# Row scalings moved to GpSimd, one weight load on ScalarE's queue, wider units for two features, and a new order

## The chip, the core and the metric

The kernel runs on one core of a Trainium2 chip. A core has five engines that work side by side and wait for each other through semaphores: TensorE (PE in the profile, with its weight loads as PEld), VectorE (DVE), ScalarE (ACT), GpSimd (POOL) and SyncE (SP), which issues most of the DMAs. The metric is the time of one execution on the device in microseconds (us). The kernel before takes 196.92 us, the median of three runs from 196.87 to 197.14.

## What is computed

The reference normalizes the rows of x (2048 x 640, bf16) and adds two branches to x: a spectral filter (a two-dimensional real FFT, a product with a complex weight, the inverse FFT) and a gated linear unit with 1536 features.

```python
xn = _layernorm(x, axis=-1)
# branch A, on xn
X = rfft2(xn)                    # 2048 x 321, complex
y = irfft2(X * (w_r + 1j * w_i))
# branch B, on xn
g = einsum("bsd,df->bsf", xn, w_gate)
u = einsum("bsd,df->bsf", xn, w_up)
z = einsum("bsf,fd->bsd", g * u, w_down)
out = x + y + z
```

## The kernel before

The 2048 rows are 16 row tiles of 128. Everything is cut into 959 small tasks. Each task has a name, an engine, and a function that emits its instructions; a table `_PLAN` (line 405) lists the tasks as triples of task number, engine (0 PE, 1 ACT, 2 DVE, 3 POOL, 4 SP) and PSUM bank. `replay` takes the table as it stands: each engine runs its tasks strictly in the listed order. `compute_waits` then adds the semaphore waits that the data, the buffers and the banks require. The durations written beside the tasks are estimates that `replay` adds up for a report and for ordering the waits; they are no instructions. So the order of each engine, and the engine of each task, are fixed by the table.

The stages, with the task names used below:

- **Normalization** (lines 731 to 798). A row tile b is loaded (`ld_x`), its mean and variance come from DVE (`bn`, `ag`, L754 and L761) or from two passes on ACT (`sm`, `sq`, L736 and L745). `sd` (ACT, L770 or L771) takes the square root, `rs` (DVE, L778) the reciprocal, for one row tile in groups 0 to 3 and for two in later ones, and `mul` (L795) writes (x - mean) * rs over the row tile in place: one instruction on 128 x 640 bf16 values.
- **Transposes**. Row tiles 0 to 3 are transposed on PE (`T0`, L814) and copied out of PSUM (`eT0`). Row tiles 4 to 15 are transposed by DMA from SP's queue (`xt`, L802), each behind its `mul`.
- **Gated unit, first half** (lines 926 to 996). A table `chunks` says which row tiles are multiplied with which features: an entry (b0, nb, f0, f1) covers nb row tiles from b0 and features f0 to f1 - 1, where one feature is a block of 128. With nb = 4 a unit is one feature with 512 columns, 5 matmuls for each of gate and up (`GU`, L951); with nb of 1 or 2 it is two features side by side, 10 matmuls of 128 or 256 columns (`GU`, L973). Two copies `eG` (ACT L681 or DVE L682) bring gate and up out of PSUM into one of three buffers, and `H` (DVE, L991 or L993) multiplies them. The weights arrive in pairs `ld_gw0_0` (gate) and `ld_gw0_1` (up), `ld_gw2_0`, and so on.
- **Forward spectral part**. On groups of 2, 2, 4, 4 and 4 row tiles DVE runs five steps `S1` to `S5` (L857 to L892), 12 instructions that combine columns of the normalized rows with two inputs from SBUF each; `S1` waits for the `mul` of all row tiles in its group and for that of the row tile behind it (row tile 3 for the first group). `R` (PE, L905) multiplies the result of a row tile, and `eR` copies it out. Then come `D` (L1034), `C` (L1053), the product with the complex weight `WM` and `SM` on DVE (L1070 to L1087), four copies with a sign `JA` to `JD` (L1100), of which `JC` and `JD` run on POOL, and `IA` (L1116).
- **Inverse part and output**. `I` (L1144), five DVE steps `V1` to `V5`, the second half of the gated unit `ACC` (L1221), which accumulates with `IV` (L1233) in one bank, and the final copies, additions and stores.

At the start PE runs 45 matmuls on constants (`warm`, L714), then `T0_0`, five more on constants (`fill0`, L704), and the first `GU`. On SP the first loads stand in this order: the first half of row tile 0 (the second half is on ACT's queue), row tile 2, row tile 1, `ld_gw0_1`, row tile 3, `ld_gw0_0`, `ld_gw2_1`, `ld_gw2_0`. On DVE the first tasks are `bn0`, `bn0`, `ag0`, `rs_0`, `mul0`, `bn1`, `bn1`, `ag1`, the two copies of `T0_0`, `rs_1`, `rs_2`, `mul1`, `mul2`. On ACT they are `sd_0`, `sm2`, `sq2`, `sd_2`, `sd_1`, `sm3`, `sq3`, `sd_3`. All sixteen `mul` run on DVE.

Of the kernel before, what the change touches and what calls it, by code (L numbers as in the profile page):

```python
# [376 lines left out]
def _d_mm(n):  # L377
    return max(n, 64) / 2.4 + 2.5
# [6 lines left out]
def _d_dve_psum(n):  # L385
    return n * 1.04 + 70.0
# [6 lines left out]
def _d_dve_tt16(n):  # L393
    return n * 0.52 + 68.0
# [6 lines left out]
def _d_act(n):  # L401
    return n * 0.833 + 62.0
# [3 lines left out]
    (11, 4, -1), (18, 2, -1), (10, 0, 2), (12, 1, -1), (0, 3, -1), (8, 3, -1), (19, 2, -1), (20, 2, -1), (21, 1, -1),  # L406
    (22, 2, -1), (23, 2, -1), (14, 4, -1), (36, 1, -1), (37, 1, -1), (38, 1, -1), (13, 4, -1), (28, 2, -1), (27, 2, -1),
    (29, 2, -1), (30, 1, -1), (24, 0, 6), (26, 2, -1), (25, 2, -1), (9, 0, 2), (31, 2, -1), (39, 2, -1), (32, 2, -1),
    (40, 2, -1), (170, 4, -1), (181, 0, 7), (15, 4, -1), (43, 1, -1), (44, 1, -1), (45, 1, -1), (33, 0, 5), (35, 2, -1),
    (34, 2, -1), (169, 4, -1), (172, 4, -1), (171, 4, -1), (16, 4, -1), (182, 1, -1), (46, 2, -1), (47, 2, -1), (41, 0, 3),  # L410
    (179, 0, 2), (180, 1, -1), (183, 2, -1), (112, 2, -1), (173, 4, -1), (174, 4, -1), (191, 0, 4), (192, 1, -1), (42, 1, -1),
    (189, 0, 1), (190, 1, -1), (48, 0, 2), (49, 1, -1), (186, 0, 5), (187, 1, -1), (196, 0, 4), (197, 1, -1), (193, 2, -1),
    (113, 2, -1), (194, 0, 7), (195, 1, -1), (62, 1, -1), (184, 0, 2), (185, 1, -1), (54, 2, -1), (53, 2, -1), (188, 2, -1),
    (17, 4, -1), (51, 2, -1), (55, 2, -1), (50, 2, -1), (52, 2, -1), (63, 1, -1), (64, 1, -1), (56, 1, -1), (114, 2, -1),
    (57, 2, -1), (198, 2, -1), (115, 2, -1), (204, 0, 3), (206, 0, 6), (65, 1, -1), (199, 0, 4), (205, 1, -1), (66, 1, -1),
    (207, 1, -1), (60, 2, -1), (116, 2, -1), (200, 1, -1), (201, 0, 7), (202, 1, -1), (203, 2, -1), (58, 2, -1), (209, 0, 0),
    (210, 1, -1), (72, 1, -1), (1, 4, -1), (211, 0, 6), (212, 1, -1), (121, 2, -1), (208, 2, -1), (67, 2, -1), (213, 2, -1),
    (119, 0, 2), (122, 2, -1), (70, 2, -1), (176, 4, -1), (175, 4, -1), (73, 1, -1), (7, 4, -1), (120, 1, -1), (117, 0, 4),
    (123, 2, -1), (216, 0, 1), (214, 0, 7), (118, 1, -1), (74, 1, -1), (217, 1, -1), (215, 1, -1), (75, 1, -1), (76, 1, -1),
    (218, 2, -1), (124, 2, -1), (68, 2, -1), (77, 2, -1), (78, 2, -1), (177, 4, -1), (221, 0, 2), (219, 0, 3), (125, 2, -1),  # L420
    (82, 1, -1), (224, 0, 0), (178, 4, -1), (220, 1, -1), (222, 1, -1), (225, 1, -1), (226, 0, 4), (227, 1, -1), (223, 2, -1),
    (83, 1, -1), (229, 0, 6), (230, 1, -1), (228, 2, -1), (130, 2, -1), (69, 4, -1), (61, 4, -1), (128, 0, 1), (129, 1, -1),
    (84, 1, -1), (231, 0, 5), (232, 1, -1), (233, 2, -1), (131, 2, -1), (85, 1, -1), (86, 1, -1), (234, 0, 4), (235, 1, -1),
    (236, 0, 2), (241, 0, 7), (242, 1, -1), (237, 1, -1), (92, 1, -1), (126, 0, 5), (239, 0, 3), (240, 1, -1), (87, 2, -1),
    (238, 2, -1), (132, 2, -1), (243, 2, -1), (133, 2, -1), (90, 2, -1), (134, 2, -1), (93, 1, -1), (94, 1, -1), (244, 0, 4),
    (59, 4, -1), (71, 4, -1), (251, 0, 1), (245, 1, -1), (95, 1, -1), (127, 1, -1), (249, 0, 0), (250, 1, -1), (96, 1, -1),
    (246, 0, 3), (247, 1, -1), (248, 2, -1), (97, 2, -1), (80, 2, -1), (254, 0, 7), (255, 1, -1), (252, 1, -1), (253, 2, -1),
    (98, 2, -1), (100, 2, -1), (88, 2, -1), (256, 0, 6), (257, 1, -1), (139, 0, 4), (141, 0, 2), (142, 1, -1), (259, 0, 0),
    (140, 1, -1), (137, 0, 1), (138, 1, -1), (3, 4, -1), (258, 2, -1), (432, 4, -1), (468, 4, -1), (431, 4, -1), (260, 1, -1),
    (143, 2, -1), (261, 0, 6), (262, 1, -1), (102, 1, -1), (263, 2, -1), (144, 2, -1), (135, 0, 3), (266, 0, 5), (267, 1, -1),  # L430
    (269, 0, 7), (264, 0, 1), (103, 1, -1), (271, 0, 2), (276, 0, 0), (104, 1, -1), (265, 1, -1), (268, 2, -1), (145, 2, -1),
    (136, 1, -1), (105, 1, -1), (270, 1, -1), (277, 1, -1), (272, 1, -1), (440, 4, -1), (274, 0, 3), (281, 0, 4), (279, 0, 1),
    (79, 4, -1), (473, 4, -1), (106, 1, -1), (273, 2, -1), (433, 4, -1), (89, 4, -1), (5, 4, -1), (434, 4, -1), (91, 4, -1),
    (2, 4, -1), (467, 4, -1), (4, 4, -1), (282, 1, -1), (107, 2, -1), (146, 2, -1), (110, 2, -1), (441, 4, -1), (101, 4, -1),
    (439, 4, -1), (435, 4, -1), (438, 4, -1), (472, 4, -1), (442, 4, -1), (286, 0, 4), (81, 4, -1), (147, 2, -1), (280, 1, -1),
    (275, 1, -1), (278, 2, -1), (108, 2, -1), (283, 2, -1), (156, 2, -1), (287, 1, -1), (284, 0, 5), (285, 1, -1), (148, 0, 2),
    (154, 0, 6), (150, 0, 0), (151, 1, -1), (149, 1, -1), (289, 0, 4), (290, 1, -1), (294, 0, 1), (295, 1, -1), (152, 0, 2),
    (291, 0, 0), (292, 1, -1), (153, 1, -1), (288, 2, -1), (296, 0, 1), (297, 1, -1), (301, 0, 4), (302, 1, -1), (157, 2, -1),
    (293, 2, -1), (158, 2, -1), (298, 2, -1), (159, 2, -1), (160, 2, -1), (299, 0, 1), (300, 1, -1), (155, 1, -1), (306, 0, 5),
    (304, 0, 0), (307, 1, -1), (305, 1, -1), (303, 2, -1), (311, 0, 1), (312, 1, -1), (309, 0, 5), (310, 1, -1), (161, 0, 3),  # L440
    (163, 0, 1), (164, 1, -1), (308, 2, -1), (162, 2, -1), (314, 0, 7), (165, 0, 4), (166, 2, -1), (315, 2, -1), (167, 0, 2),
    (316, 0, 0), (317, 2, -1), (168, 1, -1), (443, 0, 1), (446, 0, 3), (445, 1, -1), (444, 2, -1), (477, 0, 5), (447, 1, -1),
    (479, 1, -1), (321, 0, 7), (322, 1, -1), (478, 1, -1), (448, 2, -1), (313, 2, -1), (318, 2, -1), (324, 0, 1), (325, 1, -1),
    (99, 4, -1), (466, 4, -1), (109, 4, -1), (436, 4, -1), (470, 4, -1), (497, 4, -1), (437, 4, -1), (451, 0, 3), (452, 2, -1),
    (319, 0, 0), (320, 1, -1), (449, 0, 5), (450, 2, -1), (323, 2, -1), (453, 2, -1), (457, 3, -1), (455, 2, -1), (498, 4, -1),
    (469, 4, -1), (111, 4, -1), (471, 4, -1), (503, 4, -1), (474, 0, 1), (476, 1, -1), (456, 3, -1), (475, 1, -1), (502, 4, -1),
    (454, 2, -1), (326, 0, 7), (327, 1, -1), (329, 0, 0), (330, 1, -1), (505, 0, 1), (507, 1, -1), (506, 1, -1), (334, 0, 3),
    (508, 0, 6), (331, 0, 4), (510, 1, -1), (509, 1, -1), (482, 0, 1), (483, 2, -1), (336, 0, 0), (480, 0, 5), (481, 2, -1),
    (328, 2, -1), (484, 2, -1), (332, 1, -1), (335, 1, -1), (337, 1, -1), (344, 0, 7), (345, 1, -1), (536, 0, 2), (538, 1, -1),
    (537, 1, -1), (429, 4, -1), (460, 0, 1), (458, 0, 4), (341, 0, 0), (342, 1, -1), (459, 1, -1), (504, 4, -1), (333, 2, -1),  # L450
    (485, 2, -1), (486, 2, -1), (461, 1, -1), (464, 0, 7), (465, 1, -1), (462, 0, 5), (339, 0, 6), (340, 1, -1), (463, 1, -1),
    (349, 0, 0), (350, 1, -1), (501, 4, -1), (530, 4, -1), (499, 4, -1), (500, 4, -1), (511, 0, 1), (513, 0, 3), (567, 0, 6),
    (568, 1, -1), (569, 1, -1), (514, 2, -1), (512, 2, -1), (351, 0, 5), (352, 1, -1), (515, 2, -1), (516, 2, -1), (346, 0, 0),
    (347, 1, -1), (528, 4, -1), (564, 4, -1), (532, 4, -1), (430, 4, -1), (562, 4, -1), (535, 4, -1), (531, 4, -1), (559, 4, -1),
    (529, 4, -1), (561, 4, -1), (533, 4, -1), (534, 4, -1), (487, 3, -1), (488, 3, -1), (489, 0, 7), (495, 0, 6), (338, 2, -1),
    (490, 1, -1), (517, 2, -1), (594, 4, -1), (591, 4, -1), (6, 4, -1), (596, 4, -1), (539, 0, 4), (343, 2, -1), (565, 4, -1),
    (541, 1, -1), (496, 1, -1), (359, 0, 3), (491, 0, 2), (492, 1, -1), (540, 1, -1), (360, 1, -1), (493, 0, 7), (356, 0, 0),
    (357, 1, -1), (494, 1, -1), (354, 0, 2), (355, 1, -1), (544, 0, 3), (542, 0, 0), (601, 0, 5), (602, 1, -1), (603, 1, -1),
    (543, 2, -1), (366, 0, 7), (367, 1, -1), (545, 2, -1), (348, 2, -1), (546, 2, -1), (548, 2, -1), (547, 2, -1), (381, 0, 2),
# [62 lines left out]
def _build(nc, A_x, A_w_r, A_w_i, B_w_gate, B_w_up, B_w_down, out, opts=None):  # L522
    opts = opts or {}
# [821 lines left out]
```

## Time and profile before

| what | value |
|---|---|
| median of three runs | 196.92 us |
| the profiled execution | 196.79 us |
| span of its trace | 195.1 us |
| granted TensorE clock | 1.0 |
| matmuls of 128x512 in L951 | 420, mean 379 ns |
| matmuls of 128x256 and 128x128 in L973 | 160, mean 246 ns |
| `mul` (L795) on DVE | 16, mean 437 ns |
| H (L991) on DVE | 42, mean 427 ns |
| L1100 on POOL, 64x252 bf16 | 8, mean 1060 ns |
| bytes moved by DMA | 23.73 MB, mean 122 GB/s |

A mean duration in the trace is not the rate: matmuls are pipelined, so that a matmul of 512 columns is 379 ns long and passes the engine on after 216 ns, as the chain of waits shows (five in 1.08 us). The same holds for short instructions on DVE, where the next one starts some 0.08 us before the one ahead has ended. Idle time is given with the engine or DMA that ended it. Spans of POOL are rough.

### The profile page before, as it was taken

The numbers are of one execution on the slowest core, as the hardware profiler recorded it, in microseconds if no ns is written. First come the engines' busy times: TensorE is split into PE (matmuls) and PEld (weight loads), VectorE is DVE, ScalarE is ACT, GpSimd is POOL, SyncE is SP. The second block draws the span as 40 slices with busy tenths as digits, with TensorE's granted clock in tenths as the row PEclk, the third lists the DMA queues.
The fourth block names the chain that finished last, engine by engine and source line by source line (L and its number), as shares of the span: only waits on it lengthen the run. The fifth ranks groups of instructions, "written<-read, shape, count | busy, mean of one in ns | idle before, by whom it ended". The sixth has DMA issues, their size and how long they took to land.

```text
span 195.1 us, 4122 instructions
## 1 busy us (share of the span) xinstructions
PE 191.4 (98%) x1591; PEld 122.7 (63%) x1591; DVE 176.1 (90%) x367; ACT 135.9 (70%) x277; POOL 13.0 (7%) x22
## 2 busy tenths in 40 slices
PE   8899999999999999999999999999999999999995
PEld 8898644454454555555545555558777777777774
DVE  2899999999999899999989989996999999999643
ACT  3999999999767589999999999747406343332230
POOL 1000000000000000331131132030000000000000
DMA  5999725015973057167542682007001154242432
GB/s 146 322 368 331 235 53 129 7 49 123 214 142 72 3 108 212 45 169 145 140 101 59 158 275 71 0 0 200 7 3 67 43 162 134 67 134 69 135 102 67
DMA packets 29666, 23.73 MB, mean 122 GB/s; under 512 B 10448, under 2 KB 27600, under 8 KB 29520
## 3 DMA queue, kind: packets, MB, share of 16 engines
q1 hardware_dynamic: 29504, 23.41, 44.0%
q8 instruction: 12, 0.20, 0.4%
q10 hardware_dynamic: 144, 0.08, 0.2%
q14 instruction: 6, 0.05, 0.1%
HBM read 18.89 MB, written 2.62 MB: 110 GB/s over the span
## 4 chain that ended last, share of the span: by engine, by line
PE 88%; DVE 8%; ACT 1%; DMA 1%; issue 0%; ACTq 0%
PE ps L951 41%; PE ps L1221 27%; PE ps L973 6%; DVE arena L1070 3%; PE ps L905 2%; PE ps L1144 2%; PE ps L1233 2%; PE ps L1116 2%; PE ps L1034 2%; PE ps L1053 2%; DVE arena L991 1%; DMA arena<-in_A_x_dram 1%; DVE arena L1087 1%; DVE arena L1086 1%; DVE arena L1073 1%; PE ps L814 1%
## 5 line engine op out<-in xcount | busy, mean ns | idle before, releaser
L681 ACT ACTIVATE arena<-ps 128x512 bf16<-128x512 f32 (+5 forms) x215 | 112.3, 576 | 50.4 <-PE ps L1233 28.1
L951 PE MATMUL ps<-arena 128*128 128x512 bf16 x420 | 97.5, 379 | 0.0
L951 PEld LDWEIGHTS ps<-arena 128*128 128x128 bf16 x420 | 39.0, 98 | 40.4 <-ACT arena L681 0.2
L1221 PE MATMUL ps<-arena 128*128 128x320 bf16 (+2 forms) x396 | 56.9, 295 | 0.0
L1221 PEld LDWEIGHTS ps<-arena 128*128 128x128 bf16 x396 | 37.4, 98 | 13.1 <-DVE arena L682 0.2
L1070 DVE TENSOR_TENSOR arena<-ps,arena 128x256 bf16<-128x256 f32 x64 | 22.6, 415 | 2.1 <-PE ps L1053 2.0
L991 DVE TENSOR_TENSOR arena<-arena 128x512 bf16<-128x512 bf16 x42 | 17.9, 427 | 0.6
L1100 POOL TENSOR_SCALAR arena<-arena 64x252 bf16<-64x252 bf16 x8 | 8.5, 1060 | 98.1 <-DVE arena L1087 97.9
L973 PE MATMUL ps<-arena 128*128 128x128 bf16 (+1 forms) x160 | 13.8, 246 | 0.5 <-DVE arena L682 0.5
L973 PEld LDWEIGHTS ps<-arena 128*128 128x128 bf16 x160 | 12.3, 98 | 1.5 <-DMA arena<-in_B_w_up_dram 0.6
L1260 DVE TENSOR_TENSOR arena<-arena 128x640 bf16<-128x640 bf16 x15 | 7.0, 485 | 4.4 <-ACT arena L681 4.4
L1116 PEld LDWEIGHTS ps<-arena 128*128 128x128 bf16 x160 | 8.0, 117 | 3.4 <-ACT arena L681 0.2
L745 ACT ACTIVATE arena<-arena 128x640 bf16<-128x640 bf16 x12 | 10.0, 836 | 0.1
L736 ACT ACTIVATE arena<-arena 128x640 bf16<-128x640 bf16 x12 | 8.9, 740 | 0.2
L1116 PE MATMUL ps<-arena 128*128 128x64 bf16 x160 | 8.5, 198 | 0.0
L682 DVE CAST arena<-ps 128x512 bf16<-128x512 f32 (+3 forms) x11 | 7.4, 698 | 0.7 <-PE ps L905 0.6
L857 DVE TENSOR_TENSOR arena<-arena 128x768 f32<-128x768 bf16 (+1 forms) x10 | 7.9, 789 | 0.0
L1233 PE MATMUL ps<-arena 128*128 128x320 bf16 (+2 forms) x33 | 7.8, 295 | 0.0
L1034 PEld LDWEIGHTS ps<-arena 128*128 128x128 bf16 x160 | 6.3, 98 | 2.2 <-issue 0.2
L1034 PE MATMUL ps<-arena 128*128 128x64 bf16 (+1 forms) x160 | 7.0, 193 | 0.0
L1073 DVE TENSOR_TENSOR arena<-ps,arena 128x260 bf16<-128x260 f32 x16 | 6.9, 434 | 0.0
L795 DVE TENSOR_SCALAR arena<-arena 128x640 bf16<-128x640 bf16 x16 | 6.8, 437 | 0.1
(61 smaller groups left out, 183.8 us busy)
## 6 DMA issues: line engine op xcount, KB each, us to landing
arena<-in_A_x_dram SPq DMA_DIRECT2D x19, 160.0 KB, 2.6
arena<-in_A_w_r_dram SPq DMA_DIRECT2D x30, 80.2 KB, 2.5
arena<-in_A_w_i_dram SPq DMA_DIRECT2D x30, 80.2 KB, 2.4
out_dram<-arena SPq DMA_DIRECT2D x15, 160.0 KB, 1.8
arena<-in_B_w_up_dram SPq DMA_DIRECT2D x4, 320.0 KB, 6.4
arena<-in_B_w_gate_dram SPq DMA_DIRECT2D x4, 320.0 KB, 6.5
arena<-in_A_x_dram SPq DMA_DIRECT2D x1, 1280.0 KB, 9.5
arena<-c_tf SPq DMA_DIRECT2D x4, 256.0 KB, 4.0
```

What stands on the lines that cost most here:

```text
L681: return c.e.activation(dst, src, _ACTF.Copy)
L736: return c.e.activation(v_jk, v_x[:, b, :], _ACTF.Copy, scale=1.0 / _D, accum_out=v_m32[:, b:b + 1])
L745: return c.e.activation(v_jk, v_x[:, b, :], _ACTF.Square, scale=-1.0, bias=v_m32[:, b:b + 1], accum_out=v_ss[:, b:b + 1])
L951: ins = c.e.matmul(ps[:, bk, :], v_gw[:, w, j, ft, :], v_xt[:, j, rows], start=(j == 0), stop=(j == 4))
L973: ins = c.e.matmul(ps[:, bk, i * n:(i + 1) * n], v_gw[:, w, j, ft0 + i, :], v_xt[:, j, rows], start=(j == 0), stop=(j == 4))
L991: return c.e.tensor_tensor(v_ht[:, ft0, rows], gb[:, 0, :], gb[:, 1, :], _OP.mult)
L1034: ins = c.e.matmul(ps[:, bk + i, k * 64:k * 64 + n], v_uq[:, k, t + i, :], v_fd[:, k * 128 + w * n: k * 128 + w * n + n], start=True, stop ...
L1070: c.e.tensor_tensor(dst, xh, wv, _OP.mult)
L1073: return c.e.tensor_tensor(d5, x5, wt[:, :, :, 0:321:5], _OP.mult)
L1116: ins = c.e.matmul(ps[:, bk, 64 * k:64 * k + 64], yl, v_ti[:, q, 0, :], start=True, stop=True)
L1221: ins = c.e.matmul(ps[:, bk, 0:sl3.stop - sl3.start], v_ht[:, ft, a * 128:(a + 1) * 128], v_wd[:, ft, sl3], start=(ft == _FT_ORDER[0]), st ...
L1233: return c.e.matmul(ps[:, bank_of(own), 0:sl3.stop - sl3.start], v_sm[:, 2, :], v_v[:, a, sl3], start=False, stop=True)
```

## The change

The table `_PLAN` is replaced as a whole, so that the order changes on all engines. What else changes:

```diff
-        nwarm = opts.get("nwarm", 45)
+        nwarm = opts.get("nwarm", 42)
...
-                muls[b] = T("mul%d" % b, "dve", 298.0 if b < opts.get("sub_apart", 0) else 358.0, em_mul,
+                muls[b] = T("mul%d" % b, ("dve", "pool") if b >= 4 else ("dve",), {"dve": 358.0, "pool": 2800.0} if b >= 4 else {"dve": 358.0}, em_mul,
...
-                    q="sp")
+                    q="act" if w_ and i < 1 else "sp")
...
-        chunks = opts.get("chunks", ((0, 1, 0, 4), (1, 1, 0, 4), (0, 2, 4, 6), (2, 2, 0, 6), (0, 4, 6, 12), (4, 4, 0, 12), (8, 4, 0, 12), (12, 4, 0, 12)))
+        chunks = opts.get("chunks", ((0, 1, 0, 4), (1, 1, 0, 4), (2, 2, 0, 4), (0, 4, 4, 12), (4, 4, 0, 12), (8, 4, 0, 12), (12, 4, 0, 12)))
```

Beside these, three estimates of durations are altered (the load of row tile 1, `D`, `IA`) and the tasks `eG` and `H` are named by feature and row tile instead of by a running number.

Read with the task numbers resolved, the new table does the following.

- **Row scalings.** `mul5`, `mul6`, `mul7`, `mul9` to `mul13`, `mul15` and `mul14` stand on POOL, in this order, ahead of all `JC` and `JD`. `mul0` to `mul4` and `mul8` stay on DVE.
- **First weight load.** `ld_gw0_1` (320 KB) is issued by ACT, behind its half of row tile 0 and ahead of `sd_0`. SP's first loads are then row tiles 0 (half), 1, 2, 3, `ld_gw0_0`, `ld_gw2_1`, `ld_gw2_0`. Further back `ld_gw8_0` stands ahead of `ld_gw6_0`, and `xt6` is followed by `ld_fd`, `xt4`, `xt5`, `xt7`.
- **Units.** Features 4 and 5 for row tiles 0 to 3 were two units of two features with 256 columns (40 matmuls); now they are two units of one feature with 512 columns (20 matmuls).
- **Start.** On DVE: `bn0`, `bn0`, `ag0`, `bn1`, `bn1`, `rs_0`, `ag1`, `mul0`, `rs_1`, `mul1`, one copy of `T0_0`, both of `T0_1`, two `eG`, `rs_2`, `mul2`, one `H`, one `eG`, `rs_3`, `mul3`, one `H`, `S1_0`. On ACT: `sd_0`, `sd_1`, `sm2`, the other copy of `T0_0`, `sq2`, `sm3`, `sd_2`, `sq3`, `sd_3`. On PE: `T0_0`, `fill0`, `T0_1`, then `GU` of features 0 and 1 for row tile 0 (two groups) and row tile 1 (one), features 2 and 3 for row tile 0, the other group of row tile 1, `T0_2`, the other group of row tile 0, `T0_3`.
- **Between DVE and ACT.** One `eG` each of features 4, 6 and 8 for row tiles 0 to 3 goes from ACT to DVE, as do three `eG` of the first units; `eR_12`, `eR_14` and several others go the other way or change places.
- **S1 to S5.** Each group keeps its place among its neighbours on DVE to within a few `H`; the `mul` between them are gone.

## The prediction

> **What bounds the kernel now.** I read the page's busy shares and slices first, then the chain of waits, then the timeline where the chain changes hands. From the page (each digit of a row is a slice of 4.9 us, in tenths busy):
>
> ```profile
> PE 191.4 (98%) x1591; PEld 122.7 (63%) x1591; DVE 176.1 (90%) x367; ACT 135.9 (70%) x277; POOL 13.0 (7%) x22
> PE   8899999999999999999999999999999999999995
> DVE  2899999999999899999989989996999999999643
> ACT  3999999999767589999999999747406343332230
> POOL 1000000000000000331131132030000000000000
> PE 88%; DVE 8%; ACT 1%; DMA 1%; issue 0%; ACTq 0%
> ```
>
> The matmuls carry the chain, but DVE is full beside them for three quarters of the span: from 20 to 66 us the table of windows has DVE busy 45.79 of 46.00 us and PE 46.00. POOL is empty there. Of PE's own rows, from 7.07 us (first GLU matmul) to 192.81 (last matmul done) are 185.7 us, against about 184.8 us of work when I multiply each group's count by its step in the chain of waits (L951 420 x 216 ns = 90.7, L1221 52.2, L973 13.2, R and I 9.0, IA 5.4, D 4.7, C 4.4, IV 4.4, T0 0.8). So about 1 us of PE idleness is left behind 7 us. Little can be won there, and all that PE is made to wait is lost.
>
> Who would make it wait is seen at 65 us. Timeline, start and length in us:
>
> ```profile
> 65.16 0.68 DVE L892 SCALAR_TENSOR_TENSOR arena<-arena 128x512 bf16<-128x512 f32 x1
> 65.89 0.60 PEld L905 LDWEIGHTS ps<-arena 128*128 128x128 bf16 x10 [0.28 <-DVE arena L892]
> 65.95 0.72 PE L905 MATMUL ps<-arena 128*128 128x128 bf16 x10
> ```
>
> L892 is the last step of S5 for rows 12 to 15, ending 65.84; R (L905) starts 0.1 us later, its weight load having waited for it. The same holds at R_6 (S5 ends 39.71, R 39.97) and R_8 (53.66, 54.04). PE runs its list in order, so **the S1 to S5 chain on DVE is co-critical until 66 us**: if DVE falls behind by more than what it has gained, PE stops at R.
>
> **The start.** Before, in the timeline: mul0 ends 5.42, T0_0's weight load starts 5.49, copies of it on DVE end 6.92, first GLU group 7.07 (10 matmuls), T0_1 and T0_2 at 7.86, and from 8.67 PE is continuous. The new order puts bn1 ahead of rs_0 and mul0, sd_1 ahead of sm2 on ACT, a copy of T0_0 on ACT, and T0_2, T0_3 later. With the same rows' durations: bn0, ag0 as before to 4.41; bn1 4.31 to 5.19 (x1, now second on SP, lands before that: it takes x2's place, landed 3.59); rs_0, ag1 to 5.42; mul0 5.34 to 5.79; T0_0 from 5.85 (0.84 to its end, 6.69); sd_1 to 5.74, rs_1, mul1 to 6.42; T0_1 behind the fill, about 6.8 to 7.2; copies of T0_0 done at 7.1. GLU starts at 7.2, continuous if its operands come. Before, continuity started at 8.67 having already done one GLU group more (0.55) and T0_2 (0.28): comparable point 7.84. **Gain 0.64.** On ACT sq2, sm3, sd_2, sq3, sd_3 now end at 10.14 (before 9.13), mul3 10.8, T0_3 just in time at 10.85 because the two GLU groups of features 2 and 3 for row tile 0 were put ahead of it; but the copy of T0_3 ends about 12.3 and the GLU pair of rows 2 and 3 is due at 12.25, so it starts at 12.45: **minus 0.2**. Net start **-0.44**.
>
> The load on ACT's queue: gw0_1 was issued at 2.21 on SP and landed 6.47; on ACT it follows x0b's issue (ends 1.19) and frees an SP slot of 0.48. ACT's table load moves behind it, to about 1.7, and takes 1.28: done by 3.0, sd_0 is at 4.45, hidden. A rule speaks against a gain: the Trainium skill, DMA: Bandwidth & Descriptors, "Issuing engines are not separate DMA queues", says that both issuers feed the same 16 engines and only issue time is saved. By the row, a gap in the landings between x1 (4.58) and gw0_1's first (5.31) could close, and gw0_0 (8.28) come about 1 us sooner, 7.3; by the rule it gains its slots on SP, 0.57, and lands at 7.7. It is needed at 7.76. Both fit, the sum is the same; I take the rule's. Without this load's move GLU would be held to 8.3, some 0.5 us.
>
> Three warm matmuls fewer end before T0_0 anyway (45 end at 5.80 with T0_0 waiting till 5.85): 0. **512-column units**: 40 matmuls of 256 columns at 109 ns are replaced by 20 at 216: **-0.04**; H and eG counts and columns stay. Task costs and names in the diff issue nothing.
>
> **The row scalings.** The order list puts ten on POOL (rows 5, 6, 7, 9 to 15), not eight. On DVE each passes the engine on after 0.36 us (40.72, 41.08, 41.44): -3.6. The same list gives DVE three 512-column eG copies (0.61 each by the two at 68.81: +1.83) and drops one H ahead of S1_0 out of the stretch (-0.2). S1_0 starts 1.1 late (11.0 for 9.92, behind mul3 and three eG copies). So S5_4 comes 0.87 us earlier, at 64.97, **if POOL costs DVE nothing**; PE wants it 0.48 earlier. Slack: 0.4 us.
>
> No row shows a scaling on POOL. Nearest is L1100 there, 252 columns, mean 1.06 us; times 640/252: 2.7 us. From below L682's 0.40 gives 1.0. Ten back to back take 10 to 27 us between 17 and 54. Queued behind are xt6 on SP with all later loads, S1_2, S1_3, S1_4 on DVE in order. At 2.7: mul7 done 26.6 (S1_2 due 29), mul12 41.2 (behind rs_8; S1_3 due 42.3), mul14 53.5 (behind rs_9 at about 48; S1_4 due 53.6). Just in time, 0; at 4.2 us each S1_4 is 2.9 late.
>
> The dearer question is what a POOL operation does to DVE. The trace has 16, all beside DVE work. Timeline of DVE, then of POOL:
>
> ```profile
> 106.64 0.43 DVE L991 TENSOR_TENSOR arena<-arena 128x512 bf16<-128x512 bf16 x1
> 107.10 0.50 DVE L1100 TENSOR_SCALAR arena<-arena 64x1024 bf16<-64x1024 bf16 x1
> 107.63 0.96 DVE L991 TENSOR_TENSOR arena<-arena 128x512 bf16<-128x512 bf16 x2
> ```
>
> ```profile
> 106.69 1.16 POOL L1100 TENSOR_SCALAR arena<-arena 64x252 bf16<-64x252 bf16 x1 [5.45 <-DVE arena L1087]
> 107.92 0.40 POOL L682 COPY arena<-arena 64x252 bf16<-64x252 bf16 x1
> ```
>
> The DVE operation behind each POOL start is longer: L1100 0.50 for 0.42 elsewhere (+0.08), and of the two H at 107.63 the second +0.19 (a free H passes on after 0.34 and takes 0.42: 0.77 for two, not 0.96). The +0.08 (0.07 to 0.09) recurs behind nine of the other POOL operations; those that find DVE idle or reading PSUM cost nothing. The skill's SBUF — State Buffer, "Who interferes with whom", is harsher: GpSimd's only port pair is DVE's second one, and a DVE operation with two SBUF inputs and a GpSimd one that reads SBUF lock each other out for the whole instruction. All of S1 to S5 and H have two SBUF inputs. By the rule DVE loses nearly 2.7 us each, 26 us in sum. By the row, POOL let DVE in again long before its 1.16 us ended. I take the row's delay scaled by columns: 0.08 x 2.54 = 0.20 behind a wait, 0.19 x 2.54 = 0.49 for back-to-back operations; half of each, **0.34 x 10 = +3.4**, less the slack 0.4. Ends: 0.08 each (not scaled) 0.8; the rule 26.
>
> **Sum**: -0.44 - 0.04 + 3.4 - 0.4 = +2.5. The profiled span of 195.1 us becomes 197.6; with the 1.7 us around it that execution took 196.79, 0.13 below the median of 196.92, and on the median the sum gives **199.4 us**. Break-even is at 0.09 us a scaling. PE has no slack later to return it.
>
> **Rivals.**
> - A, the other side: POOL is hidden at DVE's boundaries, 0 to 0.08 each for rows 5 to 15, under the break-even: 196.92 - 0.48 + at most 0.4, so 196.5. For it: the +0.08 was the same behind the 1.16 us operation and the 0.40 us one; against: 2.5 times the columns must cross the same port.
> - B: the lock lasts with the data, much of the operation: from 1 us each, 196.9 + 9 = 206, to 222 at the rule's 26. For it: the rule; against: the 107 us rows.
> - C: POOL's results late, S1_3 and S1_4 hold DVE: decides from 2.8 us each; 4.2 gives 196.92 - 0.48 + 2.9 - 0.4 = 198.9. Two operations and two per-row scalars per element speak for it.
> - D: the start fails (T0_3's copy or gw2_1 later than worked out): +0.5 without contention, 197.4.
>
> **Chances.** Forecast (0.2 to 0.5 us each, 197.9 to 201) 0.42; A 0.30; B 0.12; C 0.10; D 0.06. A measurement tells 0.2% (0.39 us) from no change. A lies on that border: 0.24 faster, 0.06 same; D adds its 0.06 to same; the rest is slower, 0.64. Range 196.2 to 204.5: it leaves out B and the last of A.
>
> **What would show it.** POOL rows of 128x640, their mean and whether S1 (L857), S2, S3 rows beside them grow over 0.94, 1.21 and 0.68; weight loads of L905 waiting for L892 for more than 0.3; first GLU matmul near 7.2 and no PE gap to 12.2. DVE rows that stay at their length, with R unhindered, would make it wrong.

## The result, and the profile after

The changed kernel takes **202.03 us** (median of six runs, 201.42 to 203.76), the kernel before 196.89 us beside it (six runs, 196.64 to 197.14). The ratio is 1.0269, its 95% interval 1.0243 to 1.0294: **5.14 us slower**, where 2.5 were forecast.

The page of the changed kernel, with the lines that answer to those shown of before: busy times, slices (5.05 us each), granted clock, the chain of waits, and two groups (busy, mean ns, idle before):

```profile
PE 193.7 (96%) x1568; PEld 120.2 (59%) x1568; DVE 178.5 (88%) x359; ACT 137.0 (68%) x275; POOL 45.3 (22%) x32
PE   7699999998988999999999999999999999999995
DVE  2689999999999978999998998995899999998933
POOL 1001973899580000203302302330000000000000
PEclk9799999999999999999999999999999999999999
PE 55%; DVE 33%; DMA 3%; POOL 3%; issue 3%; ACT 1%; SPq 0%; DVEq 0%
L795 POOL TENSOR_SCALAR arena<-arena 128x640 bf16<-128x640 bf16 x10 | 32.2, 3229 | 26.4 <-DVE arena L778 26.4
L991 DVE TENSOR_TENSOR arena<-arena 128x512 bf16<-128x512 bf16 x44 | 19.7, 450 | 1.7 <-ACT arena L681 0.9
```

Three things are to be seen. The chain, 88% matmuls before, now has a third on DVE. PE's row shows an 8 in the tenth, twelfth and thirteenth slice, where before it had only nines. And POOL, empty there before, is busy for 3.2 us with each scaling. DVE's total went up by 2.4 us although ten scalings of 0.44 us left it (copies came); H (L991) takes 450 ns for 427.

This execution took 203.76 us, 1.7 us above the median: row tile 1 was late, PE stood for 2.1 us behind it, and was then granted half its clock from 7.4 to 10.8 us. So what follows is read from the same kernel profiled a second time at full clock: 201.47 us, span 199.7, which is 4.6 us more than before's 195.1. From 20 to 66 us, where before had PE busy for 46.00 and DVE for 45.79 us, its table of windows has (length, then PE, PEld, DVE, ACT, POOL busy, clock, DMA):

```profile
20.00:66.00 46.00, 42.91 (x235) 20.07 (x238) 45.26 (x78) 36.33 (x79) 29.65 (x10) 1.00 0.60 132
```

DVE is as full as before although ten scalings have left it; PE stands for 3.1 us. For whom, its waits say (us in total, times, longest):

```profile
PEld ps L905 <- DVE arena L892: 1.9, 2, 1.2
PEld ps L951 <- ACT arena L681: 1.7, 4, 0.7
PEld ps L951 <- DVE arena L991: 1.7, 3, 0.7
PEld ps L905 <- ACT arena L736: 1.4, 1, 1.4
```

The same view of before:

```profile
PEld ps L905 <- ACT arena L681: 1.0, 3, 0.5
...
PEld ps L905 <- DVE arena L892: 0.3, 1, 0.3
```

R (L905) waits for the last step of S5 (L892), and the gated unit waits for copies and products that stand behind DVE's work. The longest stops of PE in the second profile are these three; the others from 20 to 66 us are under 0.3 us each:

```profile
44.37 1.00 PE L905 MATMUL ps<-arena 128*128 128x128 bf16 x15 [0.94 <-DVE arena L892]
...
57.36 0.73 PE L905 MATMUL ps<-arena 128*128 128x128 bf16 x10 [0.68 <-DVE arena L892]
...
61.40 0.81 PE L951 MATMUL ps<-arena 128*128 128x512 bf16 x3 [0.60 <-DVE arena L991]
```

How DVE lost the time is seen where a scaling runs. POOL's timeline in the second profile, then DVE's (start, length):

```profile
33.78 6.66 POOL L795 TENSOR_SCALAR arena<-arena 128x640 bf16<-128x640 bf16 x2 [3.92 <-DVE arena L778]
40.73 7.51 POOL L795 TENSOR_SCALAR arena<-arena 128x640 bf16<-128x640 bf16 x2 [0.29 <-DVE arena L778]
```

```profile
37.56 0.68 DVE L876 TENSOR_TENSOR arena<-arena 128x512 f32<-128x512 f32 x1
38.16 1.20 DVE L877 TENSOR_TENSOR arena<-arena 128x512 f32<-128x512 f32 x1
39.28 0.68 DVE L878 SCALAR_TENSOR_TENSOR arena<-arena 128x512 bf16<-128x512 f32 x1
...
41.48 0.68 DVE L886 TENSOR_TENSOR arena<-arena 128x512 bf16<-128x512 f32 x1
42.09 0.93 DVE L991 TENSOR_TENSOR arena<-arena 128x512 bf16<-128x512 bf16 x1
```

One step (L877) takes 1.20 us for 0.68, and one H 0.93 for 0.41: **+0.52 us on one DVE instruction beside one scaling**, while its neighbours keep their length. Beside the ten scalings nine DVE instructions are lengthened: eight H and steps of S1, S2, S3 and S5 by 0.49 to 0.55 us, and one row scaling on DVE by 0.18; 4.31 us in sum. S5 for rows 12 to 15 ends at 69.98 us (before 65.84), and R follows at 70.13. The row names a copy on ACT as what came last, and PE had matmuls until 0.1 us before: most of PE's loss lies ahead of this R, at the stops above.

```profile
69.30 0.68 DVE L892 SCALAR_TENSOR_TENSOR arena<-arena 128x512 bf16<-128x512 f32 x1
...
70.10 0.85 PEld L905 LDWEIGHTS ps<-arena 128*128 128x128 bf16 x15 [0.40 <-ACT arena L681]
70.13 1.00 PE L905 MATMUL ps<-arena 128*128 128x128 bf16 x15
```

This first R behind the last S5 is a good mark: from it to the end of the trace are 129.1 us in before and 129.6 here.

### The profile page after: what moved, and what is told of

Read it like the earlier page. It is cut to its first block, busy times and chain, and to the rows that moved or that the text cites. A ratio compares the mean times of both kernels' runs of the same rounds, so it can differ in the third digit from the quotient of the medians.

```text
span 202.0 us, 4070 instructions
## 1 busy us (share of the span) xinstructions
PE 193.7 (96%) x1568; PEld 120.2 (59%) x1568; DVE 178.5 (88%) x359; ACT 137.0 (68%) x275; POOL 45.3 (22%) x32
## 4 chain that ended last, share of the span: by engine, by line
PE 55%; DVE 33%; DMA 3%; POOL 3%; issue 3%; ACT 1%; SPq 0%; DVEq 0%
PE ps L951 26%; PE ps L1221 16%; DMA arena<-in_A_x_dram 3%; POOL arena L795 3%; DVE arena L991 3%; DVE arena L857 3%; DVE arena L858 3%; PE ps L1116 2%; PE ps L1053 2%; PE ps L1034 2%; PE ps L973 2%; DVE arena L869 2%; PE ps L1233 2%; DVE arena L868 1%; DVE arena L1199 1%
## 5 line engine op out<-in xcount | busy, mean ns | idle before, releaser
L681 ACT ACTIVATE arena<-ps 128x512 bf16<-128x512 f32 (+6 forms) x211 | 110.9, 577 | 54.7 <-PE ps L1233 20.9
L951 PE MATMUL ps<-arena 128*128 128x512 bf16 x440 | 103.2, 379 | 0.9 <-DVE arena L991 0.8
L951 PEld LDWEIGHTS ps<-arena 128*128 128x128 bf16 x440 | 40.1, 98 | 45.1 <-ACT arena L681 1.7
L1221 PEld LDWEIGHTS ps<-arena 128*128 128x128 bf16 x396 | 37.6, 98 | 13.2
L795 POOL TENSOR_SCALAR arena<-arena 128x640 bf16<-128x640 bf16 x10 | 32.2, 3229 | 26.4 <-DVE arena L778 26.4
L991 DVE TENSOR_TENSOR arena<-arena 128x512 bf16<-128x512 bf16 x44 | 19.7, 450 | 1.7 <-ACT arena L681 0.9
L682 POOL COPY arena<-arena 64x252 bf16<-64x252 bf16 x8 | 4.3, 537 | 41.3 <-DVE arena L1087 41.1
L682 DVE CAST arena<-ps 128x512 bf16<-128x512 f32 (+4 forms) x17 | 10.7, 637 | 2.7 <-PE ps L973 1.2
L973 PE MATMUL ps<-arena 128*128 128x128 bf16 (+1 forms) x120 | 10.6, 256 | 0.0
L973 PEld LDWEIGHTS ps<-arena 128*128 128x128 bf16 x120 | 9.8, 110 | 0.4
L1116 PEld LDWEIGHTS ps<-arena 128*128 128x128 bf16 x160 | 7.6, 116 | 2.8 <-ACT arena L681 0.4
L857 DVE TENSOR_TENSOR arena<-arena 128x768 f32<-128x768 bf16 (+1 forms) x10 | 8.4, 844 | 0.3 <-POOL arena L795 0.3
L1034 PEld LDWEIGHTS ps<-arena 128*128 128x128 bf16 x160 | 6.5, 98 | 2.8 <-issue 0.3
L905 PEld LDWEIGHTS ps<-arena 128*128 128x128 bf16 x80 | 4.9, 97 | 5.2 <-DVE arena L892 1.9
L1116 PE MATMUL ps<-arena 128*128 128x64 bf16 x160 | 8.0, 198 | 0.0
```

Source lines behind the costliest of these rows:

```text
L681: return c.e.activation(dst, src, _ACTF.Copy)
L682: return c.e.tensor_copy(dst, src)
L795: return c.e.tensor_scalar(v_x[:, b, :], v_x[:, b, :], mean, v_rs[:, b:b + 1], _OP.subtract, _OP.mult)
L857: c.e.tensor_tensor(uo[:, o, :, 0:3, :], v_xb[:, b:b + nt, 0:6:2, :], v_xb[:, b:b + nt, 5:10:2, :], op)
L951: ins = c.e.matmul(ps[:, bk, :], v_gw[:, w, j, ft, :], v_xt[:, j, rows], start=(j == 0), stop=(j == 4))
L973: ins = c.e.matmul(ps[:, bk, i * n:(i + 1) * n], v_gw[:, w, j, ft0 + i, :], v_xt[:, j, rows], start=(j == 0), stop=(j == 4))
```

## The experiments

My theory: each scaling on POOL takes DVE's time (at the port that the prediction speaks of), DVE's chain to S5 is that much late, and PE pays for it. The rivals: the new order alone costs the time (more copies on DVE, a later S1); the scalings' results come late; the load on ACT's queue spoils the start. The runs, beside the kernel before in the same session (one more, of two executions, comes in the text):

| kernel | median (us) | ratio to before, 95% |
|---|---|---|
| changed, scalings on DVE | 200.71 | 1.0190 (1.0171 to 1.0209) |
| changed, first weight load on SP | 205.07 | 1.0407 (1.0372 to 1.0441) |
| changed, both of these | 202.54 | 1.0277 (1.0255 to 1.0300) |
| changed, a second time | 201.71 | 1.0247 (1.0224 to 1.0271) |
| scalings on DVE, three copies on ACT | 200.28 | 1.0182 (1.0155 to 1.0209) |
| scalings on DVE, three short copies | 199.79 | 1.0164 (1.0140 to 1.0189) |
| before, ten extra POOL operations of 640 columns | 202.28 | 1.0272 (1.0254 to 1.0291) |
| before, the same with 320 columns | 198.83 | 1.0098 (1.0081 to 1.0114) |
| before, ten extra memsets on POOL | 197.68 | 1.0040 (1.0025 to 1.0055) |
| before, six of its scalings on POOL | 199.34 | 1.0124 (1.0108 to 1.0139) |
| before, first weight load on ACT | 196.97 | 1.0015 (0.9996 to 1.0034) |

In every trace but that of the second try with both parts back (130.6), the time from the R behind the last S5 to the end is 129.1 to 129.2 us with the order of before (129.5 with six scalings moved) and 129.5 to 129.8 with the new one. So nearly all that a version costs has happened when this R starts.

**Scalings back on DVE.** The changed kernel's order, with the engine of the ten `mul` set from 3 (POOL) to 2 (DVE) in the table, each at its place in the list (60 and 68 are `mul5` and `mul6`):

```diff
-(60, 3, -1), (68, 3, -1)
+(60, 2, -1), (68, 2, -1)
...
```

> The changed kernel with its ten row scalings back on DVE, at the same places of the order list. Theory 1 (each scaling on POOL makes one DVE operation wait about 0.5 us, ten of them 4 to 5 us; on DVE they cost 3.6): DVE gains about 1.2 us net plus 0.3 of waiting for the last scaling, so 200.5 us, between 200 and 201. Rival (the scalings on POOL are a gain that the start hides): about 3 us slower than the changed kernel, 205. Rival (the start alone is at fault): no difference from 202.0.

Measured: 200.71 us (200.44 to 200.83). S5 for the last rows ends at 69.26, against 69.98 with POOL and 65.84 before. So the order alone (with the wider units and the load on ACT, which are still in) costs 3.9 us, and POOL adds 1.0 (201.71 beside 200.71): what POOL takes from DVE (4.3) is a little more than what it takes off DVE's hands (3.6). The order's part can be read from the trace: S1 begins 0.93 us later, three copies are 1.83 more and one H 0.2 less, and DVE's waits between its instructions grow by 0.72; that is 3.3 of the 3.4 us by which S5 ends later. Both the theory and its first rival hold a part.

**Extra POOL work in the kernel before.** To have POOL's price without the new order, ten operations of the scaling's kind were added to the kernel before, three behind `rs_5`, two each behind `rs_6`, `rs_7` and `rs_8`, one behind `rs_9`; they write to a place that nothing reads. The added lines shift the line numbers, by 1 up to R and by 9 behind it (L796 here is L795 of before).

```diff
+            def em_x(c, f_=5 * (i_ % 2), r_=128 * (11 + i_ // 2), m_=2 * g_ - 4):
+                return c.e.tensor_scalar(v_ht[:, f_:f_ + 5, r_:r_ + 128], v_one[:, 0:128].unsqueeze(1).to_broadcast([128, 5, 128]),
+                                         v_m32[:, m_:m_ + 1], v_rs[:, m_:m_ + 1], _OP.subtract, _OP.mult)
+            extra = T("extra%d" % i_, "pool", 2800.0, em_x,
...
```

> The kernel before with ten extra operations on POOL of the kind of a row scaling (640 columns, subtract and multiply by per-row values), which write to a place that nobody reads; the scalings stay on DVE. Theory 1 (about 0.5 us of DVE each while PE has no slack): +4.5 to +4.9 us, 201.5. If the port is held for the whole POOL operation of 3 us: over 215. If POOL is hidden, 0.08 us each: 197.4.

Measured: 202.28 us, 5.4 us more than before. POOL's group and one of DVE's (busy, mean ns, idle before):

```profile
L923 POOL TENSOR_SCALAR arena<-const-bfloat16-1.0,arena 128x640 bf16<-128x640 bf16 x10 | 35.0, 3512 | 25.0 <-DVE arena L779 25.0
...
L796 DVE TENSOR_SCALAR arena<-arena 128x640 bf16<-128x640 bf16 x16 | 9.3, 595 | 0.1
```

All order and all work of before is there, so these 5.4 us are what POOL does to DVE and what follows from it: 0.54 us for each operation. Twelve DVE instructions are longer in this trace, by 5.6 us in sum. The row scalings that stay on DVE are lengthened as well (595 ns in the mean for 437).

With half the columns (64 in place of 128 in the two slices):

> As the run with ten extra POOL operations, but of 320 columns each. Delay in proportion to the columns: half of it, +2.0 to +2.4 us, 199.1. Delay fixed per operation: as much as with 640 columns, 201.5.

Measured: 198.83 us, 2.0 us more. A DVE instruction with two inputs that is hit grows by 0.255 us in this trace, by 0.52 in the other: 0.80 and 0.81 ns a column, so its loss goes with the columns. (The scalings on DVE, with one input, grow by 0.10 to 0.13 us and by 0.31 to 0.56, which is not in proportion.) POOL's own length isn't in proportion either: 2566 ns for 320 columns, 3512 for 640. What a two-input instruction loses goes with **POOL's data**, not with the length of POOL's operation.

With a memset of the same 640 columns, which writes SBUF and reads nothing:

```diff
-                return c.e.tensor_scalar(v_ht[:, f_:f_ + 5, r_:r_ + 128], v_one[:, 0:128].unsqueeze(1).to_broadcast([128, 5, 128]),
-                                         v_m32[:, m_:m_ + 1], v_rs[:, m_:m_ + 1], _OP.subtract, _OP.mult)
+                return c.e.memset(v_ht[:, f_:f_ + 5, r_:r_ + 128], 0.0)
```

> The kernel before with ten extra memsets on POOL of 640 columns each: they write SBUF and read nothing. If DVE is held by POOL's reads alone, as with two-input operations against a reader: no change, 196.9 to 197.3 us. If POOL takes the shared ports as a whole: +3 to +5 us, as with the ten extra operations that read (202.28).

Measured: 197.68 us, 0.8 us more. Its timeline (lines shifted by 1 up to R and by 8 behind it: L796 and L999 are L795 and L991 of before):

```profile
40.61 1.60 POOL L923 MEMSET arena<- 128x640 bf16 x2 [5.04 <-DVE arena L779]
...
40.82 0.42 DVE L999 TENSOR_TENSOR arena<-arena 128x512 bf16<-128x512 bf16 x1
...
41.15 1.59 DVE L796 TENSOR_SCALAR arena<-arena 128x640 bf16<-128x640 bf16 x3
```

H, with two inputs, keeps its 0.42 us beside the memset; the three scalings take 1.59 us together for 1.15 in the kernel before. The steps of S1 to S5 beside the other memsets kept their lengths too. In the whole trace only two scalings are longer by much, 0.39 us each, and these make the 0.8 us. So what holds the steps is something that a scaling on POOL does and a memset doesn't, which fits POOL's **reads**; that a memset is also much shorter (0.69 us in the mean) was not separated from it. A scaling on DVE, which has one input, is held by a memset's writes as well.

**Part of the move in the kernel before.** Six of before's own scalings (rows 5, 6, 7, 9, 10, 11) on POOL, two of them (9 and 10) earlier in the list than they stood:

```diff
-(60, 2, -1)
+(60, 3, -1)
...
```

> The kernel before with six scalings (row tiles 5, 6, 7, 9, 10, 11) on POOL, at the same places of its order but for 9 and 10, which are put earlier; nothing else is changed. Theory (640 columns hold the port 0.52 us, and DVE saves 0.36 each): DVE loses 6 x 0.16 = 1.0 us net, PE has no slack, so 197.8 us, up to 0.5 more if a scaling on POOL is late for S1. Rival (moving scalings off DVE pays): PE sets the pace and the time stays at 196.9 or falls.

Measured: 199.34 us, 2.5 us more than before, where I expected 0.9, at most 1.4. Six operations lengthened seven DVE instructions by 3.3 us, DVE's remaining scalings among them, for 2.2 us of work taken away: 1.1 us net. The rest is not all DVE's. Two of PE's stops are behind DMAs: 0.41 us at 19.84 for a constant that landed at 19.79 (before 18.05), with which the move has nothing to do that I could find, and

```profile
36.04 5.56 PE L951 MATMUL ps<-arena 128*128 128x512 bf16 x25 [0.36 <-DMA arena<-arena]
```

for a transposed row tile. The transposes on SP stand behind `mul`s that are now on POOL, and start at 29.15 for 26.20: late results cost time here too, by another way than S1. So the move loses time without the new order as well, but the 2.5 us are not a price of POOL's hold alone.

**The copies.** If the order costs 3.9 us, its three added `eG` on DVE are the largest piece of it by duration (1.83 us). First, with the scalings on DVE, these three went back to ACT:

```diff
-(212, 2, -1)
+(212, 1, -1)
...
```

> The changed kernel with the scalings on DVE and the three copies of features 4, 6 and 8 for row tiles 0 to 3 back on ACT. Theory (DVE's chain sets the pace until R of the last row tiles, so that every copy of 0.61 us put on DVE costs its length): 200.71 - 1.83 = 198.9 us. Rival (ACT is as full as DVE between 20 and 50 us, so the copies only come late from there): no gain, 200.7 or more.

Measured: 200.28 us, 0.4 less than with them on DVE, where 1.8 were expected, and hardly clear of the spread of the runs (199.90 to 201.46, beside 200.44 to 200.83). In the traces the stretch from the first S1 to the end of the last S5 takes 57.82 us for 58.41, 0.6 less. DVE's waits name the cause:

```profile
DVE arena L991 <- ACT arena L681: 2.0, 2, 1.1
```

H of feature 4 now waits 1.1 us for its copy: ACT is full too there, busy for 5.64 of the 5.70 us up to 21.70. (Row tile 1 also landed late in this trace, at 5.18 us.) Second, the three copies were left on DVE and cut to 16 of 512 columns; the product of features 4, 6 and 8 then takes gate twice, so that up is left out of them for the first four row tiles:

```diff
-                    def em_eg4(c, gu=gu, gb=gb, u=u):
-                        return copy_on(c, gb[:, u, :], ps[:, bank_of(gu), :])
+                    def em_eg4(c, gu=gu, gb=gb, u=u, w_=16 if b0 == 0 and u == 1 and ft0 in (4, 6, 8) else 512):
+                        return copy_on(c, gb[:, u, 0:w_], ps[:, bank_of(gu), 0:w_])
...
```

> The changed kernel with the scalings on DVE, where the three copies of features 4, 6 and 8 for row tiles 0 to 3 on DVE copy 16 columns for 512; the product behind them reads gate twice, so that up is left out of these three features. No work goes to another engine. If DVE's chain sets the pace until R: about 0.5 us less each on DVE, 200.71 - 1.5 = 199.2. If it does not (PE or ACT do): 200.7.

Measured: 199.79 us, 0.9 less, where 1.5 were expected. The same stretch takes 57.43 us for 58.41, 0.98 less, and H of feature 4 waits 0.5 us for ACT; together that is the 1.5. So the copies cost DVE their duration, but not all of it can be had back: the other copy of the pair is late as well.

**The weight load.** In the changed kernel, `ld_gw0_1` was put back on SP, behind row tile 2:

```diff
-                    q="act" if w_ and i < 1 else "sp")
+                    q="sp")
...
```

> The changed kernel with the first weight load for up back on SP's queue, behind row tile 2. Theory 2 (on ACT's queue the 320 KB run ahead of row tile 1, which landed at 5.37 us and held bn1, rs_0 and mul0): row tile 1 lands before 4.4 us, mul0 ends near 5.8 for 6.84, and the time falls by about 1.1 us to 200.9. Rival (what delays row tile 1 is its own transfer, not the load beside it): it still lands after 5 us and the time stays at 202.0.

Measured: 205.07 us (203.69 to 205.90), far from what I expected, and not by the start: row tile 1 landed at 3.52, and the first GLU matmul came at 6.71. What went wrong is 50 us later. POOL with DVE's rows between:

```profile
51.03 9.02 POOL L795 TENSOR_SCALAR arena<-arena 128x640 bf16<-128x640 bf16 x2 [2.56 <-DVE arena L778]
...
55.23 1.25 DVE L891 SCALAR_TENSOR_TENSOR arena<-arena 128x512 bf16<-128x512 f32 x1
...
60.16 0.96 DVE L857 TENSOR_TENSOR arena<-arena 128x768 f32<-128x768 bf16 x1 [2.73 <-POOL arena L795]
```

The first of the two scalings, `mul15`, takes 6.54 us of the 9.02; `mul14` is done at 60.05, and S1 for rows 12 to 15, which needs it, has waited 2.73 us. This is the rival of the late results. In the second profile of the changed kernel `mul15` took 3.64 us, and the same S1 waits only 0.3 us, for a `mul14` that is done at 57.79. Yet up to `mul15` the two traces run alike, 0.22 us apart, and it starts at the same place among DVE's instructions to 0.01 us. In the one the DVE instruction that is lengthened comes 1.3 us after its start (L878 at 52.15), in the other 4.2 us after it (L891 above). What decides between the two isn't seen in the traces. All six runs with the load on SP are some 2 us or more above the changed kernel's 201.7.

With the scalings on DVE and the load on SP, that wait can't happen:

> The changed kernel with both parts back: the ten scalings on DVE and the weight load on SP's queue behind row tile 2. Against the run with the scalings alone back (200.71 us): row tile 1 can no longer be held up, but the first gate weights land later and PE waits about 0.6 us for them; DVE's chain from 13 to 69 us, not PE, decides, so 200.7 to 201.0. If the load was what made the changed kernel slow: about 199.7.

Measured: the profiled run took 201.03 us, as expected, the other four 201.79 to 202.71. A second try, expected to tell whether this spread is in the start:

> The kernel with both parts back once more (its runs went from 201.03 to 202.71, and only the first has a trace). If the first weights on SP's queue are what makes it longer than with the scalings alone back (200.71): the first gate weights land near 8 us, PE waits for them over 0.6 us, and S1_0 comes 0.3 us or more later than 10.85.

Two runs, 201.01 and 204.31 us, the profile of the longer one, with half the clock from 8.7 to 12.1 us, after a `ld_gw0_0` that landed at 8.63; so the spread isn't explained.

The load alone, in the kernel before:

```diff
-                    q="sp")
+                    q="act" if w_ and i < 1 else "sp")
...
```

> The kernel before with its first up weights issued on ACT's queue behind its half of row tile 0; the order is otherwise as before. Row tile 2 or 1 shares the DMA engines with them: row tile 1, still third, lands after 5.3 us (before 4.58), bn1 waits for it and the copies of T0_0 behind bn1 on DVE move by 0.2 to 0.5 us, so 197.0 to 197.4 us. If an empty stretch of the DMA engines is filled and nothing is held up: 196.9 or 0.1 less, since the first gate weights (8.28) come just in time already.

Measured: 196.97 us (13 runs, 196.69 to 198.59), no change that can be told. `ld_gw0_0` lands at 7.36 us for 8.28, but row tile 1 at 5.77 for 4.58, and the first GLU matmul starts at 7.49 for 7.07: what the one transfer gains is taken from the other. S5 ends at 65.99 all the same.

**The changed kernel again**, for a profile at full clock:

> The changed kernel once more, for a trace at the full TensorE clock. Row tile 1 lands at about 4.3 us as in the run with the scalings on DVE, the first GLU matmul starts near 7.1, S1_0 near 10.9; R for the last row tiles starts near 70.8, 1.4 us later than with the scalings on DVE (69.41), and the span is 200.3 us. If row tile 1 lands after 5 us here too, the start is late by over 1 us and S1_0 comes after 12.

Measured: 201.71 us (201.43 to 202.40); row tile 1 landed at 4.25, the first GLU matmul at 7.02, S1 began at 10.87, R at 70.13. It carries the accounting below.

## Why the prediction fell short

The direction and the mechanism were right: DVE's chain S1 to S5 sets R, POOL's reads take from it, and PE has no slack to give it back. The size was not: 5.1 us for 2.5. Two terms of the sum failed, POOL's hold on DVE, put too low at 3.4 us (4.31 measured), and DVE's own waits, put at nothing without a reason (0.80 measured); 0.45 us more is lost behind R, where the sum has no term. By its own terms, for the end of S5 of the last rows (before 65.84), from the second profile:

| term | forecast (us) | measured (us) |
|---|---|---|
| S1 of rows 0, 1 begins later | +1.1 | +0.95 |
| ten scalings off DVE, three copies on, one H out | -1.97 | -1.97 (the instructions that moved) |
| POOL's hold on DVE | +3.4 | +4.31 |
| waits of DVE between its instructions | 0 | +0.80 |
| not allotted | | +0.06 |
| S5 ends | 68.37 | 69.98 |

- **The start** held: -0.44 was forecast. In the second profile the first GLU matmul comes at 7.02 (7.2 forecast), and the first pair of rows 2 and 3 at 12.28 (12.45). `ld_gw0_0` landed at 7.4 to 7.9 us in the traces with this load on ACT (7.75 in the second profile; 8.28 in before), so that the rule's 7.7 and the gap's 7.3 can't be told apart; "x1 lands before that" failed in the first profile (5.37 us), where the load on the second queue delayed it:

```profile
5.40 0.89 DVE L754 BATCH_NORM_STATS2 arena<-arena 128x6 f32<-128x320 bf16 x2 [0.97 <-DMA arena<-in_A_x_dram]
...
6.89 0.28 PEld L814 LDWEIGHTS ps<-arena 128*128 128x128 bf16 x5 [2.23 <-DVE arena L795]
```

  That costs it a microsecond at the start; of the unprofiled runs nothing can be said.
- **512-column units**, -0.04: too small to be told apart in any run.
- **POOL's hold** is the first step that failed: "half of each, 0.34 x 10". The value for back-to-back operations, 0.49, was the right one. But it rested on one instruction, and the row shown for it, 0.96 us for two H, could not tell it: two H take 0.95 us with POOL empty, too. Only their own lengths tell the cases apart (timeline of before, then shortest, median and longest in ns of the two H at 107.63):

```profile
65.76 0.95 DVE L991 TENSOR_TENSOR arena<-arena 128x512 bf16<-128x512 bf16 x2
...
L991 DVE TENSOR_TENSOR arena<-arena x2: 425/521/617, 107.6 to 108.0; 128x512 bf16<-128x512 bf16 x2
```

  At 65.76 each H lasts 0.42 us and the second starts 0.10 late; at 107.63 the second is itself 0.19 longer. And nothing spoke for a half: the prediction itself had found DVE busy for 45.79 of 46.00 us, so there was hardly a wait for POOL's reads to fall into. Eight of the nine hits cost 0.49 to 0.55. Scaling by columns was right (0.255 us for 320, 0.52 for 640), and the trace had shown it at 252 columns (0.19). The Trainium skill's rule (SBUF — State Buffer, "Who interferes with whom") names the pairs as these runs show them: two-input DVE work contends with POOL's reads and is left alone by a memset. Its "whole instruction", which stands there with DVE's modes that use two ports and which the prediction carried over to two inputs, doesn't hold here: 0.52 us of 3.2.
- **DVE's own waits** are the second step that failed: they were left out of the sum. A step whose input is the instruction straight ahead loses some 0.11 us. In before a scaling stands between two such steps. First before, then the changed kernel's second profile:

```profile
51.42 0.68 DVE L886 TENSOR_TENSOR arena<-arena 128x512 bf16<-128x512 f32 x1
52.02 0.43 DVE L795 TENSOR_SCALAR arena<-arena 128x640 bf16<-128x640 bf16 x1
52.38 0.68 DVE L891 SCALAR_TENSOR_TENSOR arena<-arena 128x512 bf16<-128x512 f32 x1
```

```profile
54.82 0.68 DVE L886 TENSOR_TENSOR arena<-arena 128x512 bf16<-128x512 f32 x1
55.53 1.17 DVE L891 SCALAR_TENSOR_TENSOR arena<-arena 128x512 bf16<-128x512 f32 x1
```

  L886 passes the engine on after 0.60 us to work that doesn't need it, and after 0.71 to L891, which does. (L891's 1.17 us is once more an instruction beside a scaling on POOL.) Such gaps make 0.96 us between S1 and the last S5 in before, 1.68 with the scalings back on DVE at their new places, and 1.76 in the changed kernel, 0.33 of which is the wait for `mul14`. A version with the scalings between the steps again was not run.
- **POOL's speed**: 2.7 us forecast, 2.5 to 4.1 and 3.23 in the mean measured. The late results decide for 0.33 us in this profile, and for 2.7 us in the kernel with the load on SP.
- **"PE has no slack later to return it"** held, and a little more went: R starts 4.2 us late, the span ends 4.6 late. With the scalings on DVE the same 0.45 us is lost behind R; I did not follow it further. The rest to the medians' 4.8 and 5.1 is the spread of the runs above the profiled one.

Rival A is gone: at 0.43 us a scaling in the mean, the price is nearly five times the break-even. Rival B is gone too, for the reason given. No version that was run beats the kernel before.

## What to carry to other kernels

An engine that is full takes a neighbour's interference at its full price: where it has no idle time, price each hit at the back-to-back value, and compare that with what the moved instruction costs in place (here 0.36 us on DVE against 0.43 to 0.56 lost). When fillers are taken from between dependent steps, the steps' own latencies come out; count them. And a change of order and of engine is worth taking apart: here the order cost 3.9 of the 5 us, and the change of engine, on top of it, 1.0.

## What was not expected of the hardware

- The interference goes both ways: a scaling of 640 columns on POOL took from 2.49 us to 6.54 us. In the longest, no DVE instruction was lengthened until the first gap between DVE's instructions, 4.2 us on.
- After a stop of PE of 2.1 us at the start (first profile) and of 3.1 us before 63.7 us (load on SP), TensorE was granted half its clock for 3.4 us; in the second try with both parts back this came after stops of 0.51 and 0.75 us. After a stop of 1.25 us at the start (three copies on ACT) the clock stayed full.
- A 320 KB load on ACT's queue took row tile 1's transfer on SP's from 3.5 us (the load on SP, behind it) to between 4.25 and 5.4.
